# Chunked attention and a mish feed-forward layer: the up projection of the last 3584 tokens in Strassen's seven-product form

## The chip, the cores and the metric

The kernel runs on one core of one Trainium2 chip. A core has five engines that run side by side, each with its own queue in program order: PE (matrix products), ACT and DVE (elementwise work), POOL, and SP, which here only issues DMAs. They wait for each other through semaphores. The metric is the device time of one execution in microseconds (us); lower is better.

## The reference

```python
B, H, S, D = 8, 8, 576, 64          # attention inside chunks of 64 tokens
scores = scale * matmul(q_c, k_c.T); scores -= max(scores, -1)
attn = exp(scores); attn /= sum(attn, -1) + 1e-9
x = matmul(attn, v_c)               # as 4608 tokens x 512
h = x @ w_in                        # 512 -> 2048, the up projection
g = h * tanh(log1p(exp(h)))         # mish
out = g @ w_out                     # 2048 -> 512, the down projection
```

All tensors are float32. `x`, `w_in` and `w_out` are kept as a high part and a low part (value minus high part), so that a product of two of them is three matrix products: low times high, high times high, high times low.

## The kernel before

Tokens come in 18 pairs (`j`) of two tiles of 128 tokens; two pairs make a block of 512 tokens, so there are `NB` = 9 blocks. The inner dimension of 2048 is cut into `NF` = 16 columns of 128 (`f`). The loop runs over `N` = 144 slots, one for each block and `f`.

In a slot PE runs `up(s + 1)` (12 matrix products of 128x512: 4 pieces of the 512-long sum by 3 parts) and `down(s - 1)` (12 of 128x512: 4 token tiles by 3 parts). Between them ACT applies mish to `up`'s result, and the high and low parts of the result (`g_hi`, `g_lo`) are made. `down` adds all 16 columns of a block up in PSUM (`acc`: four halves of two tiles, `o0` and `o2`), and `store` copies them out once a block.

The attention of a pair is spread over the slots of the block ahead, by the table `plan`: scores on PE (`a_scores`), maximum and subtraction on DVE (`a_max`, `a_sub`), exponential on ACT (`a_exp`), sum and reciprocal (`a_inverse`) and scaling (`a_norm`) on DVE, a transposition on PE (`a_transpose`) with a copy on ACT, the product with v on PE (`a_values`), and the high and low parts of the result on ACT and DVE.

In the first block each slot also loads and unpacks one column of `w_in` and of `w_out` (the steps of `w`). All weights, high and low, then stay in SBUF. The order of work is written out by hand: each engine's queue follows the order of calls. Where one engine reads what another wrote, or overwrites what another still reads, the framework inserts a semaphore wait.

Of the kernel before, what the change touches and what calls it, by code (L numbers as in the profile page):

```python
# [23 lines left out]
@with_exitstack
def kernel(
# [40 lines left out]
    early = const.tile([P, 1], F32, name="early")  # L66
    wi_h = const.tile([P, NF, NK, P], F32R, name="wi_h")
    wi_l = const.tile([P, NF, NK, P], F32R, name="wi_l")
    wo_h = const.tile([P, NF, DM], F32R, name="wo_h")
    wo_l = const.tile([P, NF, DM], F32R, name="wo_l")  # L70

    w32 = {
# [39 lines left out]
    def w_dst(m, f, part):  # L116
        if m == "o":
            return (wo_h, wo_l)[part][:, f]
        return (wi_h, wi_l)[part][:, f].rearrange("p k c -> p (k c)")

# [147 lines left out]
    def a_hi(j, t=BOTH):  # L268
        b, i = divmod(j, PAIRS)
        if b not in xts:  # L270
            xts[b] = tuple(xp.tile([P, NK, TOK], F32R, name=f"{n}_{b}", tag=n) for n in ("xh", "xl"))
        nc.scalar.copy(out=x_view(j, 0, t), in_=flat(st[j]["av", t.start]))  # L272
# [14 lines left out]
    def up(i, cols=slice(0, TOK), last="x"):  # L287

        b, f = divmod(i, NF)
        xh, xl = xts[b]  # L290
# [4 lines left out]
        parts = ((wi_l, xh), (wi_h, xh), (wi_h, xl))  # L295
        for w_, x in parts if last == "x" else reversed(parts):
            for kt in range(NK):
                nc.tensor.matmul(  # L298
                    h[:, cols],
                    lhsT=w_[:, f, kt],  # L300
                    rhs=x[:, kt, cols],
                    start=(n == 0),
                    stop=(n == 3 * NK - 1),
                )
                n += 1
# [21 lines left out]
    def down(i, ts=range(TOK // P)):  # L327
        b, f = divmod(i, NF)
        d = it[i]
        for t in ts:  # L330
            if f == 0 and t == 0:
                places = [(ps_o, "o0"), (ps_o, "o2")] + ([HOME] if b == NB - 1 else [])
                o = [p.tile([P, 2, DM], F32, name=f"o_{b}_{tag}", tag=tag) for p, tag in places]

                n = len(o)
                acc.update({u: o[u % n][:, u // n] for u in range(4)} if n == 3 else
                           {u: o[u // 2][:, u % 2] for u in range(4)})
            sl = slice(t * P, (t + 1) * P)
            for n, (g, w_) in enumerate(((d["gl"], wo_h), (d["gh"], wo_l), (d["gh"], wo_h))):
                nc.tensor.matmul(  # L340
                    acc[t],
                    lhsT=g[:, sl],
                    rhs=w_[:, f],
                    start=(f == 0 and n == 0),
                    stop=(f == NF - 1 and n == 2),
                )

    def store(b, ts=range(TOK // P), end=False):

        for t in ts:  # L350
            o = wst.tile([P, DM, 2], U32, name=f"ob_{b}_{t}", tag="st", bufs=4)
            o = o.rearrange("p n t -> p (n t)")[:, :DM].bitcast(F32)
            if t % 2 and not (end and t == TOK // P - 1):
                nc.vector.tensor_copy(out=o, in_=acc[t])  # L354
            else:
                nc.scalar.copy(out=o, in_=acc[t])  # L356
# [205 lines left out]
```

## Time and profile before

| what | value |
|---|---|
| time, three runs | 877.39, 877.19, 874.45 us, median 877.19 |
| profiled execution, first to last instruction (span) | 873.7 us |
| PE, matrix products | busy 860.7 us, 99% of the span |
| PE, weight loads (beside them) | 710.0 us, 81% |
| DVE | 340.0 us, 39% |
| ACT | 258.7 us, 30% |
| DMA | 55.40 MB, mean 63 GB/s |

The profiled execution's own time is not listed beside the three runs; its span is 3.5 us under their median, which is what lies around the first and last instruction, and what runs differ by. "PE busy" counts overlapped products with modelled ends, so the step from one start to the next is the number to use. A row of the profile names line, engine, operation, output and inputs, shape and count; in brackets stands the idle time of the engine before it and what ended it.

### The profile page before, as it was taken

The page shows a single profiled execution, that of the slowest core. Times are in us where ns is not written, and L with a number is a line of the kernel's source. Part 1 is how long each engine was busy: PE and PEld are TensorE (multiplying, and loading weights), DVE is VectorE, ACT ScalarE, POOL GpSimd, SP SyncE. Part 2 cuts the span into 40 slices and gives each one's busy share as a digit, 9 for nine tenths or more (in the row PEclk, how much of TensorE's full clock was granted, in tenths as well). Part 3 has the DMA queues.
Part 4 walks back from the last instruction along what each step waited for, and adds up shares of the span by engine and source line. Part 5 has one row for each costly group of instructions (what it writes and reads, how often), then busy time and mean ns, then how long its engine had stood idle before and what let it go on. Part 6 is the DMA issues. An engine that isn't in the chain of part 4 may idle for free.

```text
span 873.7 us, 13602 instructions
## 1 busy us (share of the span) xinstructions
PE 860.7 (99%) x5984; PEld 710.0 (81%) x5984; DVE 340.0 (39%) x525; ACT 258.7 (30%) x370; POOL 0.7 (0%) x6
## 2 busy tenths in 40 slices
PE   7989999999999999999999999999999999999997
PEld 7778888888888888888888888888888888888886
DVE  6989844232424233323423242423342333322221
ACT  5988932121312122221213131212212131311111
POOL 0000000000000000000000000000000000000000
PEclk9999999999999999999999999999999999999999
DMA  7657412101310130112110131012011202002001
GB/s 290 224 163 265 144 47 51 50 25 49 73 50 25 49 73 25 50 27 58 38 64 11 48 73 49 25 49 74 25 49 49 51 24 72 1 1 49 1 0 49
DMA packets 25178, 55.40 MB, mean 63 GB/s; under 512 B 2592, under 2 KB 2592, under 8 KB 25120
## 3 DMA queue, kind: packets, MB, share of 16 engines
q1 hardware_dynamic: 24512, 53.49, 20.5%
q8 instruction: 47, 0.77, 0.4%
q10 hardware_dynamic: 608, 1.05, 0.3%
q14 instruction: 11, 0.09, 0.0%
HBM read 45.09 MB, written 9.44 MB: 62 GB/s over the span
## 4 chain that ended last, share of the span: by engine, by line
PE 96%; DVE 2%; ACT 1%; issue 0%; ACTq 0%; POOLq 0%; POOL 0%
PE h L298 44%; PE o_o L340 44%; PE s L170 2%; PE av L170 2%; PE pt L241 2%; PE o_a L340 1%; PE spare L371 1%; DVE p L232 0%; DVE r L225 0%; DVE p L211 0%; DVE m L197 0%; ACT wi_h L122 0%; DVE xl L275 0%; ACT ob L356 0%; ACT ps L251 0%
## 5 line engine op out<-in xcount | busy, mean ns | idle before, releaser
L340 PE MATMUL o_o<-wo_h,gl 128*128 128x512 f32 x560 | 223.6, 399 | 2.4 <-DVE gl L323 2.4
L318 DVE CAST gh<-z 128x512 fp32r<-128x512 f32 x128 | 54.5, 426 | 436.5 <-PE o_o L340 433.0
L310 ACT ACTIVATE z<-h 128x512 f32<-128x512 f32 x144 | 86.1, 598 | 451.6 <-PE h L298 339.6
L340 PE MATMUL o_o<-wo_h,gh 128*128 128x512 f32 x560 | 219.1, 391 | 0.0
L340 PE MATMUL o_o<-wo_l,gh 128*128 128x512 f32 x560 | 218.9, 391 | 0.0
L298 PE MATMUL h<-xh,wi_l 128*128 128x512 f32 (+1 forms) x580 | 154.4, 388 | 0.8 <-ACT xh L272 0.8
L298 PE MATMUL h<-xl,wi_h 128*128 128x512 f32 (+1 forms) x580 | 154.4, 389 | 0.0
L298 PE MATMUL h<-xh,wi_h 128*128 128x512 f32 (+1 forms) x580 | 154.2, 388 | 0.0
L298 PEld LDWEIGHTS h<-xh,wi_l 128*128 128x128 f32 x580 | 108.4, 188 | 23.3 <-ACT xh L272 0.9
L298 PEld LDWEIGHTS h<-xl,wi_h 128*128 128x128 f32 x580 | 108.6, 188 | 22.4
L298 PEld LDWEIGHTS h<-xh,wi_h 128*128 128x128 f32 x580 | 108.5, 188 | 22.3
L340 PEld LDWEIGHTS o_o<-wo_h,gl 128*128 128x128 f32 x560 | 105.4, 188 | 25.6 <-DVE gl L323 3.2
L340 PEld LDWEIGHTS o_o<-wo_h,gh 128*128 128x128 f32 x560 | 105.4, 188 | 22.2
L340 PEld LDWEIGHTS o_o<-wo_l,gh 128*128 128x128 f32 x560 | 105.5, 188 | 20.6
L323 DVE TENSOR_TENSOR gl<-z,gh 128x512 fp32r<-128x512 f32 x144 | 99.7, 692 | 14.4 <-ACT gh L316 9.9
L251 ACT COPY ps<-pt 128x1024 f32<-128x1024 f32 (+1 forms) x20 | 18.5, 927 | 81.8 <-PE pt L241 81.8
L197 DVE TENSOR_REDUCE m<-s 128x16 f32<-128x1024 f32 (+1 forms) x20 | 22.3, 1116 | 34.7 <-PE s L170 34.7
L310 ACT ACT_TABLE_LOAD x16 | 20.5, 1283 | 34.5 <-PE h L298 34.5
L354 DVE COPY ob<-o_o 128x512 f32<-128x512 f32 x17 | 11.8, 692 | 35.6 <-ACT ob L356 33.2
L170 PEld LDWEIGHTS s<-k,q 64*64 64x64 f32 x1088 | 17.9, 137 | 6.0 <-issue 5.8
L232 DVE TENSOR_TENSOR p<-p,r 128x1024 f32<-128x1024 f32 (+1 forms) x20 | 22.4, 1118 | 0.7
L220 ACT ACT_TABLE_LOAD x17 | 21.8, 1283 | 2.0 <-PEq L552 1.7
(48 smaller groups left out, 411.9 us busy)
## 6 DMA issues: line engine op xcount, KB each, us to landing
out<-ob SPq DMA_DIRECT2D x68, 128.0 KB, 2.4
wis<-in_w_in SPq DMA_DIRECT2D x16, 512.0 KB, 4.5
wos<-in_w_out SPq DMA_DIRECT2D x16, 512.0 KB, 3.8
q<-in_q SPq DMA_DIRECT2D x16, 512.0 KB, 3.6
k<-in_k SPq DMA_DIRECT2D x16, 512.0 KB, 3.7
v<-in_v SPq DMA_DIRECT2D x16, 512.0 KB, 3.9
room_v<-in_v SPq DMA_DIRECT2D x2, 512.0 KB, 8.0
q<-in_q SPq DMA_DIRECT2D x2, 256.0 KB, 3.9
```

Of the source, the lines that this page charges most:

```text
L170: nc.tensor.matmul(o[h * CHUNK : (h + 1) * CHUNK, c, t - ts.start, g], lhsT=l[rows, t, 2 * g + h], rhs=r[rows, t, 2 * g + h], start=True, ...
L197: nc.vector.tensor_reduce(out=small(j, "m", t), in_=st[j]["s", t.start].rearrange("p c t g k -> p c (t g) k"), op=ALU.max, axis=AX.X,)
L220: nc.scalar.activation(out=p, in_=p, func=AF.Exp, scale=SCALE)
L232: nc.vector.tensor_tensor(out=p, in0=p, in1=r.unsqueeze(3).broadcast_to([P, 2, r.shape[2], CHUNK]), op=ALU.mult)
L241: nc.tensor.transpose(out=d["pt", ts.start][:, t - ts.start, g], in_=d["p"][:, t, g].rearrange("p c k -> p (c k)"), identity=ident,)
L251: nc.scalar.copy(out=d["ps"][:, t].rearrange("p t h k -> p (t h k)"), in_=d["pt", t.start][:, : t.stop - t.start].rearrange("p t g n -> p ...
L298: nc.tensor.matmul(h[:, cols], lhsT=w_[:, f, kt], rhs=x[:, kt, cols], start=(n == 0), stop=(n == 3 * NK - 1),)
L310: nc.scalar.activation(out=d["z"], in_=d["h"], func=AF.Mish)
L318: nc.vector.tensor_copy(out=d["gh"], in_=d["z"])
L323: nc.vector.tensor_tensor(out=d["gl"], in0=d["z"], in1=d["gh"].bitcast(F32), op=ALU.subtract)
L340: nc.tensor.matmul(acc[t], lhsT=g[:, sl], rhs=w_[:, f], start=(f == 0 and n == 0), stop=(f == NF - 1 and n == 2),)
L354: nc.vector.tensor_copy(out=o, in_=acc[t])
```

## The change

Only the first two blocks (`PLAIN`) keep the old form. The other 3584 tokens are four blocks of 896 (`NSB`), and in them two columns `f` are taken together: `NS` = 8 column pairs, so 32 sets (`z`). The block's `x` (896 x 512) and the weight (512 x 256) are split in halves both ways, and the product is formed with seven half-size products instead of eight, from sums and differences of quarters of `x` and of the weight (Winograd's variant). A half-size product is 448 tokens by 256 by 128, in three parts: 6 matrix products of 128x448.

- The weight's seven operands are made in the second block (`t_sum`, `t_diff`, `t_hi`, `t_lo`) or written directly (`keep_weights`) to DRAM, and each set reads them back: `ring_load` (three buffers of four operands) and `wo_load` for the columns of `w_out`.
- The seven operands of `x` are made by `x_sum`, `x_hi`, `x_lo`. For the first block of 896 that is done around the last two plain slots, for each later block during the last set of the block before (`plan_x`).
- Three of the products' sums are formed in PSUM, the rest by ACT copies (`s_copy`) and DVE additions (`s_c`).
- The down projection of a set runs interleaved with the next set's products. Its 7 token tiles use the two halves of one PSUM tile `d` in turn, and each is added to a sum in SBUF by `s_out` (a DVE addition; ACT copies in the first set of a block; the last addition of a block goes to a buffer that is stored).
- The attention of pairs 4 to 7 moves to the slots 13 to 29 of the plain part (`quick`, four slots apart), that of the ten pairs after them into sets 1, 3, 5, 8, 10, 12, 14, 17, 19 and 21 (`plan_pair`).

```diff
-    NB = NT * P // TOK
+    NB = PLAIN
+    def keep_weights(f):
+        s, e = divmod(f, 2)
+        for k, half in ((0, 0), (1, 1)) if e == 0 else ((4, 1),):
+            src = w_part(f, slice(0, 2))[:, :, half * 2 * P : (half + 1) * 2 * P]
+            nc.sync.dma_start(out=raw(dwi_of(s, k)), in_=raw(src))
+        nc.sync.dma_start(out=raw(dwo[s][:, e]), in_=raw(w_part(f, slice(2, 4))))
...
+    def t_sum(s):
...
+    def t_diff(s):
...
+    def t_hi(s):
...
+    def t_lo(s):
...
+    def x_sum(b, k):
+        a11, a12, a21, a22 = (x_src(b, n) for n in (0, 1, 5, 6))
+        if k == 2:
+            xs[b] = wst.tile([P, 2, HALF], F32, name=f"xs_{b}", tag="st", bufs=4)
+        o, l, r, op = {
+            2: (xs.get(b), a21, a22, ALU.add),
+            3: (a11, xs.get(b), a11, ALU.subtract),
+            4: (a12, a12, a11, ALU.subtract),
+            5: (a21, a11, a21, ALU.subtract),
+        }[k]
+        nc.vector.tensor_tensor(out=o, in0=l, in1=r, op=op)
+    def x_hi(b, k):
+        nc.scalar.copy(out=xo[k][:, 0], in_=x_src(b, k))
+    def x_lo(b, k):
+        nc.vector.tensor_tensor(
+            out=xo[k][:, 1], in0=x_src(b, k), in1=raw(xo[k][:, 0]), op=ALU.subtract
+        )
...
+    def s_up(z, k):
+        if k == 1 and z == 0:
+            places["bg"] = ps_o.tile([P, 2, DM], F32, name="bg", tag="o0")
+        if k == 0:
+            places["a", z] = ps_h.tile([P, TOK], F32, name=f"al_{z}", tag="h")
+        o = places["bg"][:, int(k > 1)] if k in (1, 2, 4) else places["a", z]
...
+        if i == 3:
+            ring_load(g + 3)
+    def s_down(z, i):
+        if "d" not in places:
+            places["d"] = ps_o.tile([P, 2, DM], F32, name="d", tag="o2")
+        o = places["d"][:, (BT * z + i) % 2]
...
+    def s_out(z, i):
+        o = places["d"][:, (BT * z + i) % 2]
+        a = s_sum(i)
+        if s == 0:
+            nc.scalar.copy(out=a, in_=o)
+            return
+        to = a if s < NS - 1 else wst.tile([P, DM], F32, name=f"ob_{z}_{i}", tag="c")
+        nc.vector.tensor_tensor(out=to, in0=o, in1=a, op=ALU.add)
...
+    def s_c(z, n):
+        where, other = C_OF[n]
+        o = places["a", z] if where == "a" else places["bg"][:, where[1]]
+        ct[z, n] = ew.tile([P, HALF], F32, name=f"c{n}_{z}", tag="z", bufs=2)
+        nc.vector.tensor_tensor(out=ct[z, n], in0=o[:, :HALF], in1=ct.pop((z, other)), op=ALU.add)
...
+        nc.scalar.activation(out=ct[z, n], in_=src, func=AF.Mish)
+        nc.scalar.copy(out=g_view(z, n, 0), in_=ct[z, n])
+    def s_lo(z, n):
+        nc.vector.tensor_tensor(
+            out=g_view(z, n, 1), in0=ct.pop((z, n)), in1=raw(g_view(z, n, 0)), op=ALU.subtract
+        )
...
+    ORDER = (("u", 0), ("d", 0), ("u", 1), ("d", 1), ("u", 2), ("d", 2), ("u", 3), ("d", 3),
+             ("u", 4), ("d", 4), ("u", 5), ("d", 5), ("d", 6), ("u", 6))
+    def plan_set(z):
+        when(z, 0, lambda: wo_load(z), lambda: s_copy(z, "p1"))
+        when(z, 2, lambda: s_c(z, 11), lambda: s_hi(z, 11))
+        when(z, 3, lambda: s_lo(z, 11))
+        when(z, 4, lambda: s_copy(z, "p5"))
+        when(z, 6, lambda: s_copy(z, "u2"))
+        when(z, 8, lambda: s_c(z, 12), lambda: s_hi(z, 12))
+        when(z, 9, lambda: s_lo(z, 12))
+        when(z, 10, lambda: s_c(z, 22), lambda: s_hi(z, 22))
+        when(z, 11, lambda: s_lo(z, 22))
+        when(z, 13, lambda: s_hi(z, 21))
+        when(z + 1, 0, lambda: s_lo(z, 21))
+        for m, (kind, i) in enumerate(ORDER):
+            if kind == "d":
+                when(z + 1, m, lambda i=i: s_out(z, i))
+    def plan_x(z, b):
+        when(z - 1, 13, lambda: x_sum(b, 2))
+        for k, m in enumerate((0, 2, 4, 6, 8, 10, 13)):
+            when(z, m, lambda k=k: x_hi(b, k), lambda k=k: x_lo(b, k))
+        when(z, 2, lambda: x_sum(b, 5), lambda: x_sum(b, 3))
+        when(z, 4, lambda: x_sum(b, 4))
+    def plan_pair(z, j):
+        pe[z, 1] = lambda: a_scores(j)
+        when(z, 2, lambda: a_max(j), lambda: a_sub(j), lambda: load_v(j))
+        when(z, 4, lambda: a_exp(j))
+        when(z, 5, lambda: a_inverse(j))
+        when(z, 7, lambda: a_norm(j))
...
-        for s in range(N - 1):
+        for s in range(N - 2):
             slot(s)
+        x_sum(0, 2)
+        for m in range(4):
+            x_hi(0, m)
+            x_lo(0, m)
+            if m == 1:
+                x_sum(0, 5)
+                x_sum(0, 3)
+        x_sum(0, 4)
+        slot(N - 2)
+        for m in range(4, 7):
+            x_hi(0, m)
+            x_lo(0, m)
...
+        slot(N - 1)
```

For each of the 8 column pairs `t_sum` is two DVE additions of 512, `t_diff` four subtractions of 256, `t_hi` two ACT copies of 512, and `t_lo` two DVE subtractions of 512 and four DMAs. `s_copy` is one ACT copy of 448, and the two instructions of mish and copy above are `s_hi`. In the text u0 to u6 are the seven products of a set (`s_up`), d0 to d6 the token tiles of the set before (`s_down`), so0 to so6 their additions (`s_out`).

The first place is PE's queue. Before, in the middle of the seventh block, a slot is `up` (three groups of four) and `down`, whose token tiles end in two PSUM tiles, each matmul adding to what the slots before left there:

```order
L298 MATMUL h_124_6087<-xl_7_5235,wi_h_88 128x512 x4
L298 MATMUL h_124_6087<-xh_7_5234,wi_h_88 128x512 x4
L298 MATMUL h_124_6087<-xh_7_5234,wi_l_89 128x512 x4
L340 MATMUL o_7_o0_5680<-wo_h_90,gl_122_6079 128x512
L340 MATMUL o_7_o0_5680<-wo_l_91,gh_122_6077 128x512
L340 MATMUL o_7_o0_5680<-wo_h_90,gh_122_6077 128x512
```

Here is the end of set 9 now, with the start of set 10: u5, d5, d6, u6 and u0 (`al` and `bg` hold the products, `xo` an operand of x, `ring` weights from DRAM, `g` the activations, `wo` the columns of w_out):

```order
L602 MATMUL al_9_3969<-xo5_2445,ring2_2455 128x448 x6
L621 MATMUL d_2603<-wo0_2490,g0_2532 128x512 x3
L621 MATMUL d_2603<-wo0_2490,g1_2567 128x512 x3
L621 MATMUL d_2603<-wo0_2490,g0_2532 128x512 x3
L621 MATMUL d_2603<-wo0_2490,g1_2567 128x512 x3
L602 MATMUL al_9_3969<-xo6_2448,ring2_2455 128x448 x6
L602 MATMUL al_10_4093<-xo0_2387,ring2_2455 128x448 x6
```

Each token tile is now a closed sum of six that goes to the tile `d`, and d5 and d6 follow each other with no product between them.

The second place is DVE's queue. Before, in the last block but one, it has two instructions a slot (the parts of g) and now and then a step of the attention:

```order
L197 TENSOR_REDUCE m_17_0_6039<-s_17_0_5963 128x16
L318 CAST gh_121_6041<-z_121_6012 128x512
L323 TENSOR_TENSOR gl_121_6043<-z_121_6012,gh_121_6041 128x512
L211 TENSOR_TENSOR p_17_6047<-s_17_0_5963,m_17_0_6039 128x2x8x64
L318 CAST gh_122_6077<-z_122_6045 128x512
L323 TENSOR_TENSOR gl_122_6079<-z_122_6045,gh_122_6077 128x512
```

Now, in the first half of set 7, which also makes the operands of the next block (L553 is `x_sum`, L561 `x_lo`, L649 `s_out`, L669 `s_c`, L685 `s_lo`):

```order
L685 TENSOR_TENSOR g0_2532<-c21_6_3592,g0_2532 128x448
L561 TENSOR_TENSOR xo0_2387<-x32_1_2541,xo0_2387 128x896
L649 TENSOR_TENSOR sum0_2643<-d_2603,sum0_2643 128x512
L669 TENSOR_TENSOR c11_7_3623<-bg_2522,p1_7_3606 128x448
L561 TENSOR_TENSOR xo1_2390<-x32_1_2541,xo1_2390 128x896
L553 TENSOR_TENSOR x32_1_2541<-x32_1_2541 128x2x448
L553 TENSOR_TENSOR x32_1_2541<-xs_1_3595,x32_1_2541 128x2x448
L649 TENSOR_TENSOR sum0_2643<-d_2603,sum0_2643 128x512
L685 TENSOR_TENSOR g2_2660<-c11_7_3623,g2_2660 128x448
L561 TENSOR_TENSOR xo2_2395<-xs_1_3595,xo2_2395 128x896
L553 TENSOR_TENSOR x32_1_2541<-x32_1_2541 128x2x448
L649 TENSOR_TENSOR sum2_2689<-d_2603,sum2_2689 128x512
```

Between so0 and so1 stand `s_c` and three instructions of 896 columns, between so1 and so2 a subtraction and two more.

The third place is DVE's queue in a set with a pair's attention, set 10:

```order
L207 TENSOR_REDUCE m_12_0_4151<-s_12_0_4110 128x16
L221 TENSOR_TENSOR p_12_4153<-s_12_0_4110,m_12_0_4151 128x2x8x64
L669 TENSOR_TENSOR c11_10_4157<-bg_2522,p1_10_4102 128x448
L649 TENSOR_TENSOR sum0_2643<-d_2603,sum0_2643 128x512
L685 TENSOR_TENSOR g0_2532<-c11_10_4157,g0_2532 128x448
L235 TENSOR_REDUCE r_12_0_4184<-p_12_4153 128x8x2
L236 TENSOR_SCALAR r_12_0_4184<-r_12_0_4184 128x16
L237 RECIPROCAL r_12_0_4184<-r_12_0_4184 128x16
L649 TENSOR_TENSOR sum2_2689<-d_2603,sum2_2689 128x512
```

The maximum, the subtraction, the sum and the reciprocal of the attention, which before stood in slots of their own between two steps of g, now stand ahead of c11 and of so2.

More of the change, by code (lines that the diff above doesn't have):

```diff
@@ L66, with w_part, wi @@
     early = const.tile([P, 1], F32, name="early")
[L67 to L70, printed above, removed]
+    W = {}
+    def w_part(f, part):
+        if f not in W:
+            W[f] = wp.tile([P, 4, DM], F32R, name=f"w_{f}", tag="W")
+        return W[f][:, part]
+    def wi(f, part, kt):
+        return w_part(f, part)[:, kt * P : (kt + 1) * P]
     w32 = {
@@ L116, in w_dst @@
     def w_dst(m, f, part):
[L117 to L119 removed]
+        return w_part(f, part + 2 * (m == "o"))
     def w_hi(m, f):
@@ new lines, with a_x, x_src @@
+    x32 = {}
+    def a_x(j, n):
+        b, at0, ts = cols[j][n]
+        if b not in x32:
+            x32[b] = xp.tile([P, NK, 2 * HALF], F32, name=f"x32_{b}", tag="x")
+        size = (ts.stop - ts.start) * P
+        nc.scalar.copy(
+            out=x32[b][:, :, at0 : at0 + size].rearrange("p g (u k) -> p u g k", k=CHUNK),
+            in_=flat(st[j]["av", 0][:, :, ts]),
+        )
+    xo = {}
+    xs = {}
+    def x_src(b, k):
+        first, second = x32[b][:, :, :HALF], x32[b][:, :, HALF:]
+        a11, a12, a21, a22 = first[:, 0:2], first[:, 2:4], second[:, 0:2], second[:, 2:4]
+        return (a11, a12, xs.get(b), a11, a12, a21, a22)[k]
@@ new lines, with g_tile @@
+    G = {}
+    places = {}
+    def g_tile(z, e):
+        n = 2 * (z % 2) + e
+        if n not in G:
+            G[n] = wp.tile([P, 2, 2 * HALF], F32R, name=f"g{n}", tag="W")
+        return G[n]
+    def s_up(z, k):
[4 more added lines that the diff above has]
+        o = places["bg"][:, int(k > 1)] if k in (1, 2, 4) else places["a", z]
+        g, i = divmod(7 * z + k, 4)
+        w_, x = ring[g % 3][:, i], xo[k]
+        n = 0
+        for wn, xn in ((1, 0), (0, 0), (0, 1)):
+            for kt in range(2):
+                nc.tensor.matmul(
+                    o[:, :HALF],
+                    lhsT=w_[:, wn, kt * P : (kt + 1) * P],
+                    rhs=x[:, xn, kt],
+                    start=(n == 0 and k < 3),
+                    stop=(n == 5),
+                    skip_group_check=True,
+                )
+                n += 1
+        if i == 3:
+            ring_load(g + 3)
@@ L503, in slot @@
             a_inverse(a["exp"])
+        if "max" in e:
+            a_inverse(e["max"])
         if "x" in a:
             a_lo(a["x"])
+        if "v" in e:
+            a_x(e["v"], 0)
         if a.get("load", 0) > PAIRS:
             load_qk(a["load"])
+        if "load" in e:
+            load_qk(e["load"])
         if "max" in a:
             load_v(a["max"])
+        if s < NF and s > 0:
+            keep_weights(s - 1)
+        if s == NF:
+            keep_weights(s - 1)
+        if 0 <= tset < NS:
+            if part == 0:
+                t_sum(tset)
+                t_diff(tset)
+            else:
+                t_hi(tset)
+                t_lo(tset)
```

220 lines of the change are left out of this document (194 added, 26 removed).

## The prediction

> **What bounds the kernel now.** I read the page first, then the waits, the stretches of the steady part, and single instructions.
>
> ```profile
> span 873.7 us, 13602 instructions
> PE 860.7 (99%) x5984; PEld 710.0 (81%) x5984; DVE 340.0 (39%) x525; ACT 258.7 (30%) x370; POOL 0.7 (0%) x6
> ```
> ```profile
> DVE gh L318 <- PE o_o L340: 433.0, 119, 5.6
> ...
> PE o_o L340 <- DVE gl L323: 2.4, 1, 2.4
> ```
> ```profile
> 784.13 0.39 PE L340 MATMUL o_o<-wo_h,gl 128*128 128x512 f32 x1
> ...
> 785.26 0.39 PE L340 MATMUL o_o<-wo_h,gh 128*128 128x512 f32 x1
> ...
> 785.69 0.59 ACT L356 COPY ob<-o_o 128x512 f32<-128x512 f32 x1 [0.71 <-PE o_o L340]
> ...
> 786.31 0.69 DVE L354 COPY ob<-o_o 128x512 f32<-128x512 f32 x1 [3.48 <-ACT ob L356]
> ...
> 786.62 0.39 PE L340 MATMUL o_o<-wo_h,gh 128*128 128x512 f32 x1
> 786.85 0.62 PE L298 MATMUL h<-xl,wi_h 128*128 128x512 f32 x2
> 787.05 0.59 ACT L356 COPY ob<-o_o 128x512 f32<-128x512 f32 x1 [0.77 <-PE o_o L340]
> ```
>
> PE is the bound: 99% busy, and DVE waits 433 us for it while it waits 2.4 us for DVE. So whatever takes PE time off shortens the kernel, if nobody makes PE wait. The step from matmul to matmul is the currency: from 784.13 to 786.85 twelve start, 0.2267 us each. The same list shows how PSUM is guarded. The copy of the first half of a two-half tile, on ACT, starts at 785.69, when the second half's last matmul (785.26 + 0.39) is over, three matmuls after its own; and DVE's copy of the second half waits for ACT's copy of the first, although they share no byte. Waits go by the tile, not by its half.
>
> **The gain.** Shorter matmuls need a step at 448 columns; the first `up` in the prologue gives 256:
>
> ```profile
> 26.00 0.64 PE L298 MATMUL h<-xh,wi_h 128*128 128x256 f32 x4
> 26.48 1.57 PE L298 MATMUL h<-xl,wi_h 128*128 128x256 f32 x8
> ```
>
> Four take 0.48, 0.120 each; on the line through 256 and 512 a step at 448 is 0.200 us, weight loads included. Before, 7 x 16 x 12 = 1344 matmuls of `up` fall to these tokens; now 32 x 42 = 1344, each 0.0267 shorter: **-35.9 us**. `down` keeps 1344 of 512, and the attention's work on PE stays. A product u is 1.20 us, a token tile d 1.36, a set 7 x 2.56 = 17.9.
>
> **What it adds beside PE.** Prices:
>
> ```profile
> L323 DVE TENSOR_TENSOR gl<-z,gh 128x512 fp32r<-128x512 f32 x144 | 99.7, 692 | 14.4 <-ACT gh L316 9.9
> L310 ACT ACTIVATE z<-h 128x512 f32<-128x512 f32 x144 | 86.1, 598 | 451.6 <-PE h L298 339.6 <-issue 105.6 <-DVE p L211 6.2
> L318 DVE CAST gh<-z 128x512 fp32r<-128x512 f32 x128 | 54.5, 426 | 436.5 <-PE o_o L340 433.0 <-ACT p L220 3.5
> L220 ACT ACT_TABLE_LOAD x17 | 21.8, 1283 | 2.0 <-PEq L552 1.7
> L211 DVE TENSOR_TENSOR p<-s,m 128x1024 f32<-128x1024 f32 x16 | 19.5, 1217 | 0.0
> L225 DVE TENSOR_REDUCE r<-p 128x16 f32<-128x1024 f32 x16 | 19.4, 1215 | 0.0
> L220 ACT ACTIVATE p<-p 128x1024 f32<-128x1024 f32 x16 | 17.0, 1062 | 0.2
> L272 ACT CAST xh<-av 128x1024 fp32r<-128x1024 f32 x16 | 16.2, 1014 | 6.7 <-PE av L170 6.7
> L316 ACT CAST gh<-z 128x512 fp32r<-128x512 f32 x16 | 9.8, 612 | 2.3 <-PE o_o L340 2.3
> L227 DVE RECIPROCAL r<-r 128x16 f32<-128x16 f32 x16 | 4.0, 253 | 0.5
> L226 DVE TENSOR_SCALAR r<-r 128x16 f32<-128x16 f32 x16 | 2.8, 175 | 0.5
> ```
> ```profile
> 51.87 0.68 DVE L323 TENSOR_TENSOR gl<-z,gh 128x512 fp32r<-128x512 f32 x1
> ...
> 52.61 0.50 PE L340 MATMUL o_o<-wo_h,gl 128*128 128x512 f32 x1 [2.39 <-DVE gl L323]
> 52.95 0.39 PE L340 MATMUL o_o<-wo_l,gh 128*128 128x512 f32 x1
> ```
>
> A two-operand DVE instruction is 0.69 at 512 and 1.22 at 1024, by the line 0.63 at 448 and 1.09 at 896; on ACT a copy is 0.56 and 0.91, mish 0.55. A plain set loads DVE with 7 (`s_c`, `s_lo`) x 0.63 + 7 x 0.69 = 9.2 of 17.9, so the mean has room. The places don't.
>
> *A. d6 after d5.* By the tile rule d6 waits for so5, the reader of the other half; the built program agrees (the count that its semaphore wait asks for is the one that DVE reaches with so5). The loop: matmul to reader 0.20 (786.85 to 787.05), so5 0.69, DVE's end to PE 0.06 (52.55 to 52.61), and a first step of 0.34 instead of 0.23: 1.06 us. The other tiles have a product of 1.20 between them, which just covers it while DVE is free. 31 sets have a down projection, three of them are in C: 28 x 1.06 = **29.7** (25 to 35).
>
> *B. A pair's attention.* Scores take 1.09 us (the rows below). In a set that began at 0, d0 ends at 2.6, scores 3.7, DVE's maximum 5.1, subtraction 6.3, c11 6.9; u2 writes the tile `bg` that c11 reads and was ready at 6.2: 0.9 with the restart. Then ACT: mish and copy of c11 to 8.0, table 9.3, exponential 10.4; DVE's sum and reciprocal 12.1, so2 12.8. d3 waits for so2 and was ready at 10.8: 2.2. Seven such sets at 3.1, three (1, 8, 17; part of the readers on ACT) at about 2: **27.7** (20 to 33).
>
> ```profile
> 29.80 1.16 PE L170 MATMUL s<-k,q 64*64 64x64 f32 x64
> 30.89 1.19 PE L298 MATMUL h<-xl,wi_h 128*128 128x512 f32 x4
> ```
>
> *C. Operands of the next block (sets 7, 15, 23).* DVE gets 11 more instructions of 1.09, so 21.2 in a set of 17.9, and in the queue shown they stand ahead of the `s_out` that PE waits for. `x_lo` also waits for `x_hi`, which stands on ACT behind mish. DVE's ends, from u0's start: x_lo0 4.0, so0 4.7, c11 5.3, x_lo1 8.4 (x_hi1 ready at 7.3), two sums 10.6, so1 11.3, lo11, x_lo2, sum 14.1, so2 14.8, x_lo3, so3 17.2, c12 18.3, x_lo4 21.4 (ACT 20.3), so4 22.1, lo12, c22, x_lo5 26.5, so5 27.2. PE: d1 waits 1.0, d2 4.0, d3 and d4 1.2, d5 2.0, d6 3.7; it ends at 29.9 instead of 17.9. 3 x 12.0 = **36** (24 to 40).
>
> *D. The passage.* Eight of 1.09 and g's two stand on DVE ahead of down(30), 9.8 us against the 5.4 of up(31) and down(29), with DVE half a microsecond behind already: PE waits 5. Then 3.1 of `t_sum` and `t_diff`, three of 1.09 and g's two against down(30) and u0: 3.5. In set 0, u2 waits 1.2 and u6 2.2 behind the last `t_lo` and the stores. Three of the early pairs transpose 0.8 late behind `t_lo`. **14.3** (9 to 17).
>
> *E. The end.* The last seven tiles have no products between them: six more loops of 1.06 and a little: **6.8** (4 to 9). What follows the last matmul stays (868.50 to the span's end, 5.2).
>
> ```profile
> 868.50 0.39 PE L340 MATMUL o_o<-wo_h,gh 128*128 128x512 f32 x1
> ```
>
> *F. The clock.* After the gap of 2.39 us at 52.61 the granted clock was lower for a stretch:
>
> ```profile
> 53.00:64.00 11.00, 11.00 (x47) 9.00 (x46) 9.28 (x16) 9.47 (x17) 0.00 (x0) 0.84 0.63 191
> ```
>
> Sixteen hundredths of 11 us are 1.8 us lost. Longer gaps than that one come 8 times (two in D, two in each set of C); at most 14, partly hidden where PE next waits for DVE anyway: **8** (0 to 14).
>
> *G. DMA in the first block.*
>
> ```profile
> 8.00:18.00 10.00, 7.61 (x170) 6.78 (x170) 8.81 (x18) 7.44 (x11) 0.00 (x0) 1.00 1.04 400
> 31.00:98.00 67.00, 64.61 (x397) 52.78 (x398) 58.55 (x89) 58.41 (x98) 0.00 (x0) 0.97 0.65 208
> ```
>
> `keep_weights` adds 0.92 MB a slot, 11.0 in the twelve slots of 31 to 98, to 13.9 that are moved there: 372 GB/s against 400 seen. It just fits: **2** (0 to 18; the high end below). Later a set reads 2.9 MB in 19 us, 152 GB/s, a set or more ahead: nothing. [...]
>
> *Sum.* 29.7 + 27.7 + 36 + 14.3 + 6.8 + 8 + 2 = 124.5, less 35.9: +88.6. The sum is made against the span of 873.7, which gives 962; the median of the runs is 3.5 above the span, so 877.2 + 88.6 = **966 us**.
>
> **Rivals.**
> *R1, waits go by the half.* The two halves of `d` alternate; if d6 waited for so4 only, A and E nearly vanish, B falls to 0.4 a pair, a set of C to about 8, F to 5: 4 + 24 + 13 + 2 + 5 + 2 = 50, so 877.2 + 14 = 891. For it speaks the alternation in the code, against it the copies at 785.69 and 786.31. [...]
> *R2, faster: DVE's slack covers it.* Before, 340 us of DVE cost PE 2.4. If so_i were never the last to arrive, only D and G remain: 877.2 - 35.9 + 16.3 = 858. It decides if every reader may be 2.6 us late (one u and one d); by the walk above the slack is 0.1.
> *R3, the DMAs bind the first block.* In the stretch with a store the traffic was 53 GB/s at a share of 0.24, 221 at full share:
>
> ```profile
> 780.00:800.00 20.00, 20.00 (x90) 16.54 (x89) 5.77 (x10) 2.97 (x5) 0.00 (x0) 1.00 0.24 53
> ```
>
> If the writes to DRAM go at that rate, 13.9 / 0.40 + 11.0 / 0.221 = 85 us instead of 67: 966 + 16 = 982.
>
> **How the numbers follow.** The forecast 0.80, R1 0.08, R2 0.03, R3 0.09. Half a per cent (4.4 us) is what a measurement here can tell from no change; only R2 is faster (0.03), the low end of R1 within it (0.02), the rest slower (0.95). The terms' bounds give 923 to 1000 if all err one way; a range of 8 in 10 is 938 to 990, and R3 lies in it.
>
> **What would show it.** PE busy falls below 90%. d waits for L649 on DVE some 40 times or more, most near 1 us and once in each set but the first; the longest waits, 3 to 5, near slot 30 and in sets 7, 15 and 23. Matmuls of 448 start 0.200 apart, sets without attention take 19.0, sets 7, 15 and 23 about 30 to 32, with the granted clock under 1 in them. Wrong would be: no wait at d6 (R1), a PE share of 99% (R2), steps of 448 no shorter than 0.227, or waits for DMAs in the first block (R3).

## The result

The changed kernel takes 981.4 us (979.8 to 984.0), the kernel before 877.3: a ratio of 1.120, 95% interval 1.117 to 1.123. The forecast was 966 with 938 to 990; it is right in sign and range and 15 us short. The profiled execution took 984.0 us, with a span of 982.2. Single executions of the kernels of experiments 5 and 6 and of the kernel before took 1181, 1670 and 1230 us, up to twice as long as the others of the same kernel, and the times given below leave them out.

First the page of the kernel after, then its waits of PE (engine, line, what it waits for: us in total, times, longest):

```profile
span 982.2 us, 14424 instructions
PE 875.6 (89%) x5984; PEld 719.2 (73%) x5984; DVE 532.1 (54%) x802; ACT 426.0 (43%) x669; POOL 0.7 (0%) x6
```
```profile
PE d L621 <- DVE sum L649: 57.2, 43, 3.6
PE d L621 <- DVE ob L649: 14.5, 12, 5.0
PE bg L602 <- DVE c L669: 7.5, 11, 3.5
PE o_o L346 <- DVE gl L333: 6.1, 2, 3.5
...
PE s L180 <- issue: 2.4, 1, 2.4
```

PE was 99% busy and is 89% busy, with the same number of matmuls. It still waits for DVE, which is busy only 54% of the span: a wait for an engine that has time, but not at that moment. The two lines of `d` waiting for L649 (`s_out`, into `sum` or `ob`) hold 72 us in 55 waits.

The timeline of PE in set 2, a plain set, shows the loop of term A and the step of the short matmuls:

```profile
289.89 1.54 PE L621 MATMUL d<-wo,g 128*128 128x512 f32 x6
291.27 1.38 PE L602 MATMUL al<-xo,ring 128*128 128x448 f32 x6
292.48 1.54 PE L621 MATMUL d<-wo,g 128*128 128x512 f32 x6
294.81 1.67 PE L621 MATMUL d<-wo,g 128*128 128x512 f32 x6 [0.79 <-DVE sum L649]
296.32 2.59 PE L602 MATMUL al<-xo,ring 128*128 128x448 f32 x12
```

Six matmuls of 448 columns take 291.27 to 292.48 = 1.21 us, 0.20 each as forecast. d6, the fourth row, starts 2.33 after d5 instead of 1.38.

The next rows are from set 7, which also makes the next block's operands (u6 of set 6 starts at 385.71, u6 of set 7 at 417.12):

```profile
391.50 1.65 PE L621 MATMUL d<-wo,g 128*128 128x512 f32 x6 [0.59 <-DVE sum L649]
...
397.94 2.82 PE L621 MATMUL d<-wo,g 128*128 128x512 f32 x6 [3.58 <-DVE sum L649]
...
405.58 1.66 PE L621 MATMUL d<-wo,g 128*128 128x512 f32 x6 [0.58 <-DVE sum L649]
...
409.89 1.65 PE L621 MATMUL d<-wo,g 128*128 128x512 f32 x6 [1.44 <-DVE sum L649]
414.73 2.59 PE L621 MATMUL d<-wo,g 128*128 128x512 f32 x6 [3.19 <-DVE sum L649]
```

The two long waits are at d2 and d6, where the walk of term C had them (4.0 and 3.7). The 2.82 us behind the first of them, for the 1.65 of the others, is the lower clock: 0.52 was granted from 397.94 to 400.80.

How long a set lasts, from the start of u6 to the next u6 in the traces (us):

| | plain (26 to 30) | with a pair (12) | 7 | 16 | 24 |
|---|---|---|---|---|---|
| after | 19.2 | 25.25 | 31.4 | 25.8 | 23.2 |
| forecast for it | 19.0 | 25.0 | 29.9 | 19 | 19 |
| `d` in two tiles | 18.1 | 22.1 | 22.8 | 19.2 | 19.2 |
| no operands | 19.2 | 25.3 | 19.2 | 24.9 | 21.1 |
| light pairs | 19.2 | 22.6 | 31.1 | 25.7 | 21.2 |
| order alone | 19.2 | 25.3 | 20.5 | 25.0 | 21.3 |
| tiles and order | 18.1 | 21.6 | 18.1 | 18.1 | 18.1 |

The rows from the third on are the experiments. The lengthening of sets 16 and 24 was not forecast at all: the forecast has them as plain sets. Set 24 also differs between executions: it lasts 23.2 in after, but 21.1 or 21.2 in experiments 2, 3 and 10, and the edits of 3 and 10 do not touch it.

### The profile page after: what moved, and what is told of

Its sections match the earlier page's. It is cut to its first block, busy times and chain, and to the rows that moved or that the text cites. A ratio compares the mean times of both kernels' runs of the same rounds, so it can differ in the third digit from the quotient of the medians.

```text
span 982.2 us, 14424 instructions
## 1 busy us (share of the span) xinstructions
PE 875.6 (89%) x5984; PEld 719.2 (73%) x5984; DVE 532.1 (54%) x802; ACT 426.0 (43%) x669; POOL 0.7 (0%) x6
## 4 chain that ended last, share of the span: by engine, by line
PE 64%; DVE 16%; ACT 9%; DMA 5%; issue 5%; SPq 1%; POOLq 0%; DVEq 0%; ACTq 0%; POOL 0%
PE d L621 28%; PE al L602 14%; PE bg L602 8%; PE o_o L346 4%; PE h L308 3%; DVE sum L649 3%; DMA wos<-in_w_out 2%; DVE xo L561 2%; PE s L180 2%; DMA out<-ob 2%; DVE m L207 2%; PE av L180 2%; DVE c L669 2%; PE pt L251 2%; ACT c L681 1%
## 5 line engine op out<-in xcount | busy, mean ns | idle before, releaser
L621 PE MATMUL d<-wo,g 128*128 128x512 f32 x1344 | 362.1, 405 | 76.8 <-DVE sum L649 57.2
L621 PEld LDWEIGHTS d<-wo,g 128*128 128x128 f32 x1344 | 252.0, 191 | 148.9 <-DVE sum L649 74.5
L649 DVE TENSOR_TENSOR sum<-d,sum 128x512 f32<-128x512 f32 x168 | 115.6, 688 | 141.8 <-PE d L621 141.7
L602 PE MATMUL al<-xo,ring 128*128 128x448 f32 x768 | 179.2, 376 | 1.9 <-DVE c L669 1.9
L602 PEld LDWEIGHTS al<-xo,ring 128*128 128x128 f32 x768 | 148.4, 195 | 19.7 <-DVE c L669 2.3
L602 PE MATMUL bg<-xo,ring 128*128 128x448 f32 x576 | 137.4, 375 | 7.5 <-DVE c L669 7.5
L685 DVE TENSOR_TENSOR g<-c,g 128x448 fp32r<-128x448 f32 x128 | 79.3, 620 | 91.4 <-ACT g L682 91.4
L602 PEld LDWEIGHTS bg<-xo,ring 128*128 128x128 f32 x576 | 108.6, 191 | 25.5 <-DVE c L669 12.1
L308 PE MATMUL h<-x,w 128*128 128x512 f32 (+1 forms) x396 | 94.6, 389 | 0.8 <-ACT x L282 0.8
L346 PE MATMUL o_o<-w,gh 128*128 128x512 f32 x256 | 81.8, 402 | 0.0
L561 DVE TENSOR_TENSOR xo<-x,xo 128x896 fp32r<-128x896 f32 x24 | 25.9, 1091 | 37.7 <-ACT xo L558 37.7
L660 ACT COPY u<-al 128x448 f32<-128x448 f32 x32 | 17.1, 534 | 57.2 <-PE al L602 57.0
L649 DVE TENSOR_TENSOR ob<-d,sum 128x512 f32<-128x512 f32 x28 | 19.3, 690 | 36.1 <-PE d L621 26.7
L669 DVE TENSOR_TENSOR c<-bg,u 128x448 f32<-128x448 f32 x32 | 20.0, 624 | 32.0 <-PE bg L602 32.0
```

What stands on the lines that cost most here:

```text
L308: nc.tensor.matmul(h[:, cols], lhsT=wi(f, w_, kt), rhs=x[:, kt, cols], start=(n == 0), stop=(n == 3 * NK - 1),)
L346: nc.tensor.matmul(acc[t], lhsT=g[:, sl], rhs=w_part(f, w_), start=(f == 0 and n == 0), stop=(f == NF - 1 and n == 2),)
L561: nc.vector.tensor_tensor(out=xo[k][:, 1], in0=x_src(b, k), in1=raw(xo[k][:, 0]), op=ALU.subtract)
L602: nc.tensor.matmul(o[:, :HALF], lhsT=w_[:, wn, kt * P : (kt + 1) * P], rhs=x[:, xn, kt], start=(n == 0 and k < 3), stop=(n == 5), skip_gro ...
L621: nc.tensor.matmul(o, lhsT=g_tile(z, e)[:, gn, i * P : (i + 1) * P], rhs=wos[z % 2][:, e, wn], start=(n == 0), stop=(n == 5),)
L649: nc.vector.tensor_tensor(out=to, in0=o, in1=a, op=ALU.add)
```

## The experiments

**1. `d` in two tiles.** The theory: PE waits because a PSUM wait goes by the tile. The rival: DVE is late anyway.

```diff
-        if "d" not in places:
-            places["d"] = ps_o.tile([P, 2, DM], F32, name="d", tag="o2")
-        o = places["d"][:, (BT * z + i) % 2]
+        n = (BT * z + i) % 2
+        if ("d", n) not in places:
+            places["d", n] = ps["o"].tile([P, DM], F32, name=f"d{n}", tag=f"d{n}")
+        o = places["d", n]
...
```

> The two halves of d become two PSUM tiles of their own; nothing else is changed. If waits go by the tile (the forecast's reading), d(i+1) no longer waits for so(i): A (29.7) and E (6.8) go, B falls from 27.7 to about 4, C from 36 to about 24, F loses some 3: 75 us, so 981 becomes about 906 (895 to 920), plain sets last 18.0 instead of 19.2, pair sets about 21.7 instead of 25.3, and the waits of d for L649 (57 us) nearly vanish. The rival, that DVE is simply late whatever the tile, lets d wait for the same instructions one tile later: less than 15 us come back, 966 or more, plain sets stay at 19.

Measured: 896.7 us (ratio to before 1.022, 1.019 to 1.025), 84.7 less than after. Its waits of PE:

```profile
PE d L624 <- DVE sum L652: 13.5, 12, 1.8
PE o_o L347 <- DVE gl L334: 7.3, 3, 3.5
PE bg L604 <- DVE c L672: 4.6, 11, 0.7
```

57.2 us of waits of `d` became 13.5, and a plain set fell by 1.08, the loop's price of 1.06. In the same place of set 2, d5 and d6 are one unbroken row:

```profile
291.56 1.38 PE L604 MATMUL al<-xo,ring 128*128 128x448 f32 x6
292.77 2.90 PE L624 MATMUL d<-wo,g 128*128 128x512 f32 x12
```

DVE does the same instructions in the same order, so the rival falls. The gain is 10 us larger than expected: sets 7, 15 and 23 fell by 26 us together and not by 12 and some clock, and sets 16 and 24 fell too, by 6.6 and 4.0. Against that, the passage to the sets got 2.8 us longer: the two new tiles take the place of those of the plain part, and u1 of set 0 waits 4.6 us for one of that part's copies.

**2. No operands for the next block.**

```diff
-        if s == NS - 1 and b + 1 < NSB:
-            plan_x(z, b + 1)
```

> Blocks 1 to 3 reuse block 0's sums of tokens as operands: the preparation of the next block's operands (x_hi, x_lo, x_sum) is left out of sets 7, 15 and 23, so the output is another. If term C is right, these sets fall from 31.4 to the 19.3 of a plain set: 36 us, and 3 to 8 of half clock after their gaps: about 940 (932 to 946). Rival: the sets are long because the down projection and the loads of 2.9 MB are late there anyway, not for DVE's queue: under 12 us.

Measured: 941.4 us (1.073, 1.070 to 1.076), 40.0 less. By stretches (window: length, busy time of PE, PEld, DVE, ACT and POOL with their counts, granted clock, DMA share, GB/s), set 7 of after and set 7 here:

```profile
385.70:417.10 31.40, 22.02 (x85) 17.20 (x84) 18.77 (x24) 11.20 (x17) 0.00 (x0) 0.91 0.30 106
```
```profile
383.60:402.80 19.20, 18.42 (x85) 15.69 (x84) 8.93 (x14) 6.15 (x11) 0.00 (x0) 1.00 0.48 175
```

DVE's work falls by 9.8 us in this window, the set by 12.2, and the clock is whole. Sets 7, 15 and 23 give 36.1 us together, the sets behind them 4.1 (2.1 of it in set 24, which differs by as much without this edit). Term C holds; loads and the down projection are not what makes those sets long.

**3. Pairs without DVE's work.**

```diff
-        when(z, 2, lambda: a_max(j), lambda: a_sub(j), lambda: load_v(j))
-        when(z, 4, lambda: a_exp(j))
-        when(z, 5, lambda: a_inverse(j))
-        when(z, 7, lambda: a_norm(j))
+        when(z, 2, lambda: load_v(j))
+        when(z, 4, lambda: exp_of_scores(j))
```

> In the ten sets with a pair, DVE's maximum, subtraction, sum, reciprocal and normalisation are left out; ACT takes the exponential straight from the scores in PSUM (the softmax is not normalised, so the output is another). If B is right, d3 no longer waits for so2 behind them and u2 not for c11: pair sets fall from 25.3 to about 22.2 (scores 1.1, transposes and values 1.9 stay on PE), 25 to 30 us in all: about 953 (948 to 960). Rival: the pair sets are long for PE's own attention work and the exponential on ACT: under 10 us.

Measured: 957.4 us (1.091, 1.086 to 1.096), 24 less. `exp_of_scores` is ACT's exponential, straight out of PSUM. In after, set 12 has the two waits of term B, at u2 and d3:

```profile
515.76 1.48 PE L602 MATMUL bg<-xo,ring 128*128 128x448 f32 x6 [0.36 <-DVE c L669]
517.08 1.55 PE L621 MATMUL d<-wo,g 128*128 128x512 f32 x6
518.47 1.37 PE L602 MATMUL al<-xo,ring 128*128 128x448 f32 x6
521.64 1.65 PE L621 MATMUL d<-wo,g 128*128 128x512 f32 x6 [1.79 <-DVE sum L649]
...
530.15 1.66 PE L621 MATMUL d<-wo,g 128*128 128x512 f32 x6 [0.78 <-DVE sum L649]
```

Here is d3 of the same set without them:

```profile
504.54 1.54 PE L621 MATMUL d<-wo,g 128*128 128x512 f32 x6
```

Both waits are gone and only d6's stays, and the set lasts 22.6. What this pair costs beyond its own time on PE is 2.7 us, and it is DVE's. The ten sets gain 24 together: sets 1, 8 and 17, where ACT does part of the reading, only 1.9 of it, sets 10 and 19 4.3 each, of which some 1.6 is the slow clock behind the gap (below).

**4. The stores on another queue.** The waits of `ob` for its store were not in the forecast; the first guess was the queue, where the stores stand behind loads.

```diff
-                queue = nc.scalar if z == NSB * NS - 1 and e else nc.sync
+                queue = nc.scalar if z == NSB * NS - 1 and e else nc.gpsimd
```

> The stores of sets 8, 16, 24 and 32 go out on the GpSimd queue instead of behind the loads of ring, w_out, q and k on the sync engine's queue. If the waits of ob for its store (9.4 us of DVE, a cost that the forecast left out) come from that queue, sets 16 and 24 fall from 25.8 and 23.2 to 20 or 21 and the end gets a little shorter: 8 to 12 us, about 971 (967 to 975). Rival: with two buffers the 2.6 us to landing and the DMA engines' load set the wait: under 3 us.

Measured: 980.1 us (1.118, 1.114 to 1.122): no change, and set 16 lasts 25.7. The guess falls. The rows of POOL, SP and DVE in set 16 here:

```profile
620.61 1.03 POOL L654 DMA_DIRECT2D out<-ob  x2 [1.56 <-DVE ob L649]
```
```profile
620.83 0.32 SPq L574 DMA_DIRECT2D ring<-dwi  x1
621.24 0.39 SPq L162 DMA_DIRECT2D q<-in_q  x1
621.73 0.45 SPq L162 DMA_DIRECT2D k<-in_k  x1
```
```profile
627.35 0.69 DVE L649 TENSOR_TENSOR ob<-d,sum 128x512 f32<-128x512 f32 x1 [3.23 <-DMA out<-ob]
```

The store that left on its own queue at 620.61 frees its buffer at 627.35, 6.7 us later, where such a store lands in 2.6 to 2.7 us in the median. 2 MB of loads were issued within a microsecond of it. So the queue is not what holds the store back; that it meets the loads in the DMA engines themselves is the author's estimate, and no run shows it.

**5. One-bank tiles everywhere.** As experiment 1, and `bg` too, and the four halves of the plain part. One-bank is the name here for a tile of one half, 512 float32 columns.

```diff
-                o = [ps_o.tile([P, 2, DM], F32, name=f"o_{b}_{tag}", tag=tag) for tag in ("o0", "o2")]
-                acc.update({u: o[u // 2][:, u % 2] for u in range(4)})
+                acc.update({u: bank["p"].tile([P, DM], F32, name=f"o_{b}_{u}", tag=f"o{u}") for u in range(4)})
...
-            places["bg"] = ps_o.tile([P, 2, DM], F32, name="bg", tag="o0")
+            places["bg", k - 1] = bank["p"].tile([P, DM], F32, name=f"bg{k - 1}", tag=f"o{k - 1}")
```

> Only the one-bank PSUM tiles, all else as in the changed kernel. By the tile rule u2 no longer waits for c11, and u1 in set 0 for one store only: 4.6 + 0.7 in set 0 and 0.36 with the restart in ten pair sets, 9 us under the 896.7 of splitting d alone: 888 (883 to 892). Rival: those waits are hidden behind others: within 3 us of 896.7.

Measured: 884.0 us (1.010, 1.008 to 1.012), 97 less than after and 13 less than experiment 1.

**6. Tiles and order together.** Experiment 5, and the 18 instructions for a block's operands spread (each entry below: set, step, operation, operand):

```diff
+    X_ORDER = (
+        (-1, 13, x_sum, 2), (0, 0, x_hi, 0), (0, 0, x_lo, 0), (0, 2, x_hi, 1), (0, 3, x_sum, 5),
+        (0, 5, x_lo, 1), (0, 5, x_hi, 2), (0, 7, x_sum, 3), (0, 7, x_hi, 3), (0, 8, x_lo, 2),
+        (0, 11, x_sum, 4), (0, 11, x_hi, 4), (0, 11, x_hi, 5), (0, 11, x_lo, 3), (0, 13, x_hi, 6),
+        (0, 13, x_lo, 4), (1, 3, x_lo, 5), (1, 4, x_lo, 6),
+    )
...
+        when(0, 11, lambda: t_sum(NS - 1), lambda: t_diff(NS - 1))
+        when(0, 13, lambda: t_hi(NS - 1), lambda: t_lo(NS - 1))
```

Those of the first block are spread over slots 30 and 31 and set 0 likewise, and the last seven outputs get buffers of their own.

> Seven products kept, three things put right together: every PSUM tile is one bank (both halves of bg and of d apart, from the first down projection on); the operands of the next block are prepared one instruction a step, the last two in the following set, and those of the first block likewise; the last weight sums move into set 0 and the last seven outputs have buffers of their own. If tile-wide waits and the order in DVE's queue are the cause, then from the 896.7 of d alone: sets 7, 15 and 23 from 22.8 to 18.5 (13 us), the waits of bg in set 0 and in ten pair sets 8, the passage 5, the end 2, half clock 4: about 865 (858 to 873), that is 1 to 2% faster than the kernel before, with 448-column steps of 0.200 as the only gain. Rival: DVE's load of 21 us in a set of 18 is the cause, not its order: those sets stay at 21.5 or more, and the time at 878 or more.

Measured: 858.3 us, a ratio of 0.980 to the kernel before (0.978 to 0.982): 2% faster than before, and 123 us faster than after. Its page, its waits of PE, and sets 7 and 8 together, in after and here:

```profile
span 858.8 us, 14422 instructions
PE 836.2 (97%) x5984; PEld 711.1 (83%) x5984; DVE 529.5 (62%) x802; ACT 423.7 (49%) x669; POOL 0.7 (0%) x6
```
```profile
PE s L182 <- issue: 4.5, 2, 2.7
PE o L347 <- DVE gl L335: 2.6, 1, 2.6
PE pt L253 <- DVE p L244: 2.5, 5, 1.2
PE bg L603 <- ACT p L669: 2.2, 1, 2.2
PE al L603 <- DVE c L678: 2.1, 1, 2.1
```
```profile
385.71:441.50 55.79, 44.89 (x306) 36.00 (x304) 34.30 (x46) 22.53 (x33) 0.00 (x0) 0.94 0.46 154
```
```profile
363.78:403.70 39.92, 39.80 (x305) 34.09 (x303) 33.74 (x47) 22.30 (x33) 0.00 (x0) 1.00 0.63 221
```

DVE is as busy as in after (529.5 and 532.1 us), and PE hardly waits for it. Two of the operands' instructions now stand in set 8 and no longer in set 7, so the two sets have to be taken together: with some 34 us of DVE's work in both kernels they last 39.9 instead of 55.8, and PE has no gap. So the load on DVE was not the limit in these sets.

Of the 35.9 us that the shorter products were to bring, 17 come out. In the profiled execution most of the rest stands in three places: 6 to 7 for the changes between lengths (below), 4.5 in gaps "issue", and 4.3 in two waits of set 0.

**7. The order alone.** The edit of experiment 6 without that of experiment 5: `d` and `bg` stay as in after.

> The changed kernel with the spread operands, the moved last weight sums and the buffers of the end, but with bg and d as tiles of two halves. If tiles and order were independent causes, the order brings what it brought on one-bank tiles, 885.3 - 859.1 = 26 us: 955 (950 to 960). If each instruction that stands ahead of so_i on DVE costs double where d(i+1) waits for so_i, as the walk of term C has it, sets 7, 15 and 23 fall from 31.4 to about 21, the sets after them by 2, the passage by 5: 940 (934 to 948). Rival: with tile-wide waits the order hardly matters: 970 or more.

Measured: 937.7 us (1.072, 1.070 to 1.073), 43.6 less. Sets 7 and 8 together:

```profile
375.47:419.52 44.05, 41.32 (x306) 33.69 (x304) 34.10 (x46) 22.50 (x33) 0.00 (x0) 1.00 0.57 196
```

They fell from 55.8 to 44.1 with the same work on DVE, set 7 alone from 31.4 to 20.5. The three such sets give 32 us, the passage most of the rest. This is the walk's reading and not the sum of independent causes: on one-bank tiles the same order brings 884.0 - 858.3 = 26.

**8. The control: the kernel before on one-bank tiles.** The edit of experiment 5 on the kernel before; its last block, which had a third tile for its sums, gets the four tiles too.

> A control: the kernel before (no seven-product form) with the same one-bank PSUM tiles. There TensorE waits 2.4 us for DVE in all, so the tile rule costs nothing to be had back: within 2 us of 877 (875 to 879). Rival: the gain of the best version is partly one that the kernel before could have had from its PSUM tiles as well: 4 us or more below 877.

Measured: 877.2 us, a ratio of 1.001 (0.999 to 1.002). The tiles alone are worth nothing there; so the 2% of experiment 6 belong to the seven products.

**9. The clock.** In sets 7, 15 and 23 PE gets matmuls that do nothing for the output, in the two long gaps: `fill` is 20 products of 128x128 into an idle PSUM tile.

```diff
+                if z % NS == NS - 1 and z < NSB * NS - 1 and i in (2, 6):
+                    fill(z, i)
                 s_down(z - 1, i)
```

> The changed kernel, with 20 matmuls of 128x128 (0.122 us each in the prologue, 2.4 in all) on an idle PSUM tile ahead of d2 and of d6 in sets 7, 15 and 23, in the two gaps of 3.6 and 3.2 us; the result of these matmuls is not used. If the gaps bring the half clock (term F), the half-clock windows in these sets vanish; since TensorE next waits for DVE anyway, a window costs only part of its 1.7 us: 0 to 8 us less, 973 to 981. Rival 1: the windows come from elsewhere and stay, the time as well (within 2 us of 981). Rival 2: the filling delays d2 and d6: 983 or more.

Measured: 979.6 us (1.119, 1.116 to 1.121), 1.9 less, by the whole times not told from nothing; the trace says more. Set 7 by stretches, and its rows around d2, on PE and on DVE:

```profile
384.20:414.80 30.60, 27.97 (x166) 24.49 (x165) 18.68 (x24) 11.20 (x17) 0.00 (x0) 1.00 0.31 110
```
```profile
392.73 4.63 PE L854 MATMUL fill<-ident 128*128 128x128 f32 x40
397.12 1.63 PE L621 MATMUL d<-wo,g 128*128 128x512 f32 x6
```
```profile
395.72 0.69 DVE L649 TENSOR_TENSOR sum<-d,sum 128x512 f32<-128x512 f32 x1
```

The granted clock is 1.00 instead of 0.91: no gap, no slow stretch. The expectation had the filling's price wrong: the trace writes a product of this kind as two records, so 20 took 4.4 us and not 2.4, and d2 came 0.7 us after so1's end at 396.41, and d6 1.0 late. The three sets are 2.3 us shorter together, in spite of some 5 us of such delay. So the slow clock costs about 7 us in these three sets by this estimate; what the run shows directly is 2.3.

**10. The weights written later.**

```diff
-        if s < NF and s > 0:
-            keep_weights(s - 1)
-        if s == NF:
-            keep_weights(s - 1)
+        if s > NF:
+            keep_weights(s - NF - 1)
+        if s == N - 1:
+            keep_weights(NF - 1)
```

> The weights are written to DRAM in the second block's slots instead of the first's, so the first block's 31 to 98 us carry 11 MB less. By term G (2 us) the first store comes 0 to 3 us earlier and the whole gains 0 to 3: 978 to 982. Rival (R3 at a lower price): the writes hold up the loads in the first block: 6 us or more less there, 975 or below.

Measured: 979.3 us (1.119, 1.116 to 1.121), 2.1 less, which with these intervals is not told from nothing. The first block from 31 to 98 us, in after and here:

```profile
31.00:98.00 67.00, 64.39 (x456) 52.27 (x455) 55.51 (x84) 55.26 (x92) 0.00 (x0) 0.97 0.97 323
```
```profile
31.00:98.00 67.00, 64.40 (x397) 52.46 (x396) 58.68 (x89) 58.38 (x98) 0.00 (x0) 0.97 0.62 205
```

The DMA share falls from 0.97 to 0.62 and PE's busy time does not move: a full DMA share bound nothing. R3 falls.

## Why the prediction was right, and where it was short

What it said would show came: PE below 90%, `d` waiting for L649 more than 40 times, steps of 0.200, sets of 30 to 32 with a clock under 1. Two signs came otherwise: plain sets last 19.2 and not 19.0, and the longest wait of `d`, 5.0 us, stands in set 16, where none was forecast. Its mechanism is shown: PE waits where DVE's read of one half of a PSUM tile holds up the write into the other, and wherever something stands ahead of that read in DVE's queue. Splitting the tiles takes 97 us off, the order alone 44, both 123. The terms, one by one, in us:

| | forecast | measured | from |
|---|---|---|---|
| A, d6 after d5 | 29.7 | 28 x 1.08 = 30 | 19.2 less 18.1 a plain set |
| B, pairs | 27.7 | 21 | 24 less the 3 of clock in sets 10 and 19, experiment 3 |
| C, operands | 36 | 36: 40 less 7 of clock, plus 3 for d6, which experiment 2 keeps in these sets | experiments 2 and 9 |
| D, passage | 14.3 | 9.8 | waits of 3.5, 3.5, 1.9, and 0.3 at three transposes |
| E, end | 6.8 | 6.7 | below |
| F, clock | 8 | some 15: 7 in C, 3 in sets 10 and 19, 5 in the passage | experiment 9 and the rows below |
| G, DMA in the first block | 2 | 2.1, give or take 3 | experiment 10 |
| stores of sets 16 and 24 | none | 5.7 and 1.9 | experiment 2's row less 19.2 |
| changes between the two matmuls | none | 0.2 a set, 6 to 7 | 18.1 less 17.9 |
| PE's gap "issue" in the prologue | none | 2.4 in the profiled run | waits |

E is the stretch from u6 of set 30 to the span's end: 41.3 us in after and 33.4 with tiles and order, less the 1.08 of d6 in set 31. The split alone brings 4.0 of this (36.2 in experiment 1), the buffers of the last outputs without it nothing (41.3 in experiment 7). The table's lines add up to 137; less the gain of 35.9 they give 101 of the 108.5 between the two spans. The last 7 us are not placed. Between the spans the forecast of 88.6 is 20 short, and that is a balance: B and D were set 11 too high, what was set too low, left out or is not placed makes some 31. So the range was hit partly by luck; the sign was not, since A, B and C alone outweigh the gain more than twice. The upper bounds of the terms add up to 1007, not to the 1000 that the forecast gives.

So no step failed in kind, but the sum left out three things. The largest is the stores, 7.6 us: with two buffers, `ob` waits for a store, one of which was out for 6.7 us among 2 MB of loads (experiment 4), and since `s_out` is what d waits for, DVE's wait for a DMA became PE's (5.0 us, in the waits above). DVE's row in set 16 of after:

```profile
631.36 0.69 DVE L649 TENSOR_TENSOR ob<-d,sum 128x512 f32<-128x512 f32 x1 [4.95 <-DMA out<-ob]
```

The forecast had looked at loads that are "a set or more ahead" and taken the DMAs of the later sets for nothing. On split tiles the same kind of wait costs PE nothing: experiment 6 keeps two buffers for these sets, waits 7.8 us on DVE, and sets 16 and 24 last 18.1. The second is the 0.2 us a set for the 14 changes between matmuls of 448 and 512, some 0.015 each (291.27 - 289.89 = 1.38 for six steps of 0.2267 = 1.36). The third is the gap in the prologue, which comes and goes with the execution (last section).

D was set too high: the wait of 5 before down(30) measured 3.5, and the one of 3.5 behind it did not come, while u2's 1.2 in set 0 came as 3.5. B was too high mainly in sets 1, 8 and 17 (1.9 instead of 6 together). F is the term that was mis-sized most. The count of 8 gaps was too low, because shorter ones bring the slow clock too. Here are d3 and u4 in set 10, the stretch of the passage, and the core's mean clock:

```profile
475.28 1.83 PE L621 MATMUL d<-wo,g 128*128 128x512 f32 x6 [1.80 <-DVE sum L649]
476.91 2.44 PE L602 MATMUL bg<-xo,ring 128*128 128x448 f32 x6
```
```profile
225.00:257.00 32.00, 22.97 (x126) 18.21 (x129) 17.02 (x27) 13.61 (x23) 0.00 (x0) 0.84 0.71 248
```
```profile
core 0: 982.2 us, clock 0.974
```

Six products take 2.24 us in set 10 (476.91 to 479.15, where the next d starts) instead of 1.21, and the sets 10 and 19 that have such a stretch last 26.9 instead of 25.3. In the passage 0.16 x 32 = 5 us of clock are lost. The mean clock of 0.974 over 982 us is 25.5 us lost in all, three times the forecast's F; some 15 of them are in the table. Of the other 10, some 3 fall in sets 7, 15 and 23 where PE next waits for DVE, as the forecast had it; 3.4 lie around the wait of 5.0 in set 16, and 3.4 in the prologue and the first block, of which the kernel before has 1.7 too.

The rivals: R1 (waits by the half, 891) is not what the changed kernel does, but it priced the split well: the kernels that split the halves measured 896.7 and 884.0. As the two halves of one tile, `d` kept PE waiting for `sum` for 57.2 us, as two tiles for 13.5 (experiment 1): different halves were not enough for the waits, they had to be different tiles. R2 (858, no reader is ever late) is not the changed kernel either, and tiles and order together, which come near that state, take 858.3. That the two agree so closely is in part chance: R2 pays 14.3 for the passage, of which experiment 6 has some 4 left, and nothing for the changes between lengths. R3 fell with experiment 10; that its 982 is the time that was measured is chance.

## What to carry to other kernels

An engine that is half idle can still hold up the bound one (here DVE, busy 54%, held PE up for 72 us): look at what each wait guards, by tile, and at what stands ahead of the awaited instruction in its queue, before you count busy time. Give each half of a PSUM tile that another engine reads while the next is written a tile of its own (97 us here), and spread added work one instruction a step (44 us here, 123 with the tiles), so that a shorter product is not paid back in waits. Where an output buffer is read by a slow DMA, its wait can go through to whoever waits for the engine that fills it: here 4.95 us of DVE became 4.98 of PE.

## What the hardware showed beside that

The slow clock does not follow from the gap's length alone: after the wait of 1.80 us in set 10 the next products run at half rate, after that of 1.79 in set 12 (shown above, 521.64 with the usual 1.65) they don't. In after, all slow stretches begin whole multiples of 3.413 us apart, the first four at 19.20, 56.75, 227.42 and 244.48: 11, 50 and 5 steps. Here are the steps of this grid that hold the wait of set 10 and what follows it, and the two that share the wait of set 12:

```profile
473.18:476.59 3.41, 1.61 (x8) 1.09 (x7) 3.10 (x5) 1.98 (x3) 0.00 (x0) 1.00 0.05 15
476.59:480.00 3.41, 3.41 (x10) 2.87 (x9) 1.23 (x2) 0.00 (x0) 0.00 (x0) 0.50 0.00 0
517.55:520.96 3.41, 2.29 (x11) 1.68 (x9) 1.59 (x5) 3.21 (x5) 0.00 (x0) 1.00 0.16 26
520.96:524.37 3.41, 2.73 (x13) 2.39 (x14) 2.44 (x4) 0.75 (x1) 0.00 (x0) 1.00 0.75 288
```

PE was busy for 1.61 us, 47%, of the step with set 10's wait, and the next step ran at half clock; set 12's wait is divided between two steps that were busy for 67% and 80%, and the clock stayed whole. The rest of the trace fits: of its steps at full clock, each of the 14 in which PE was busy for under 48% was followed by a slow one at 0.50, and none of the 258 with over 48%. In the trace of before the two steps under 45% (39%, and 0% at its end) were each followed by a slow one, and none of the 252 over 51%. So in these two traces what counts is how much of a step is idle, and a gap's place decides that as much as its length.

The gap that the profile calls "issue", in the scores of the prologue, differs from execution to execution: 2.4 us in after, 0.84 in experiment 4, none in experiments 1, 9 and 10. The control has one of 2.7 us, so it is not the seven-product form that brings it; later scores of the plain part have such gaps too (2.2 us in experiment 1). What causes them stays open.
